# Local and strided attention with two feed-forward layers on one core: attention blocks 1 to 6 in another order, and the first weight conversions moved by a block

## The chip, the cores and the metric

The kernel runs on 1 core of one Trainium2 chip. The metric is device time in microseconds (us) of one execution. A median over runs is given for the kernel before; the profile comes from one execution whose own time is given beside its span.

## The reference

Three layers follow each other. Only the first lines matter here, since the change sits in the attention and in what the first feed-forward layer starts on.

```python
scores = scale * np.matmul(q, k.transpose(0, 1, 3, 2))      # batch 4, 8 heads, 576 positions, 64 wide
mask_local = (rel >= 0) & (rel < 32)                         # heads 0 to 3
mask_strided = (rel >= 0) & (pos[None, :] % 32 == pos[:, None] % 32)   # heads 4 to 7
attn = np.exp(scores - np.max(scores)); attn = attn / (np.sum(attn) + 1e-09)
x = matmul(attn, v)                  # becomes 2304 tokens x 512
h = x @ w_in;  g = h * np.tanh(softplus(h));  x = g @ w_out            # 512 -> 2048 -> 512
out = (silu(x @ w_gate) * (x @ w_val)) @ w_out2                        # 512 -> 1536 -> 512
```

## The kernel before, in words

**Precision.** The matrix products of the two feed-forward layers are done in three parts. Each operand is held as a high part (a cast, on ScalarE, L105) and a low part (the operand less its high part, on VectorE or GpSimd, L110). `mm3` (L112) issues three matmuls: high by high, high by low, low by high. Such a group is called a triple here. The low part of the weight is read by the third matmul only, and the low part of the input by the second only.

**Weights.** The weights arrive as 64-bit numbers and are converted. One weight tile takes four steps (`w_ops`, L195): a (a Square on ScalarE, L237, and a shift on VectorE, L238), b (L241), c (L244) and d (L247). Step d also asks for the next raw tile over SP's queue (`w_load`, L157). Then `w_hi` (L184) casts the high part on ScalarE and `w_lo` (L176) subtracts the low part on VectorE. `w_step(n)` (L255) issues the next n of these steps. The four tiles 0 to 3 hold the first quarter of `w_in`.

**Attention.** There are 24 steps (L297), each with six or eight blocks of 64 queries for two heads at once. Steps 0 to 2 and 6 to 8 are local (96 keys), steps 3 to 5 strided (64 keys). The work of a step is spread over four blocks of the program, which run as a pipeline: block a (`at_pair`, L537) issues scores (`at_qk`, TensorE), minima (`at_max`, VectorE) and exponentials (`at_exp`, ScalarE) of step a; sum and normalisation of step a-1 (`at_add`, `at_norm`: a reciprocal on VectorE, the rest on GpSimd); transposes and their copies of step a-2 (`at_tr`, `at_copy`); the product with v, the cast and the low part of step a-3 (`at_pv`, `at_hi` on ScalarE, `at_lo` on VectorE). What `at_hi` and `at_lo` write is x, the input of the first feed-forward layer. Minima, exponentials, transposes and copies come in two halves. The product with v has one PSUM buffer, so `at_pv` of a step waits for `at_lo` of the step before it; the scores have one pair of buffers, so `at_qk` waits for the minima of the block before.

**The order.** Every engine runs its instructions in the order of the program. The list `PAIR` (L506) gives the order within a block: load, transposes and copy of the first half, add, norm, product with v, load of v, `at_hi`, `at_whi` (the weight cast), scores, minima and exponentials of the first half, `at_conv`, `at_lo`, minima, transposes, copy and exponentials of the second half, `at_wlo` (the low part of the weight). For the blocks in `SC_FIRST` (1, 2, 3) the five entries in `SCORES` (L528) come first. Copies of the first half go to ScalarE for steps 2, 3 and 4 (`COPY_ACT`) and to VectorE otherwise; those of the second half always go to ScalarE.

**Between the blocks.** Behind block k the loop at L896 issues `KEEP[k]` filler matmuls on zeros (`spin`, L860; four of them behind blocks 2, 3 and 4), then `WSTEPS[k]` conversion steps, then the triples listed in `GROUPS[k]`. A triple (n, f, kc) belongs to column tile f of part n of the first layer and takes rows kc of x, which is head pair kc: head pairs 0 and 1 come from steps 0 to 2, 2 and 3 from steps 3 to 5. For n = 0 it reads weight tile f // 2 + 2 (kc // 2): tile 0 is read by the triples (0, 0 or 1, 0 or 1), tile 1 by (0, 2 or 3, 0 or 1), tile 2 by (0, 0 or 1, 2 or 3), tile 3 by (0, 2 or 3, 2 or 3).

Of the kernel before, what the change touches and what calls it, by code (L numbers as in the profile page):

```python
# [46 lines left out]
for _f in (0, 2):  # L47
# [26 lines left out]
}  # L74
CONV_FIRST = {3: 4}
COPY_ACT = (2, 3, 4)
WSTEPS = (0, 0, 0, 0, 4, 4, 2, 2, 1, 1, 2, 2, 2, 2, 2)
WFILL = 4
PAIR_AT = (0, 14, 17, 20, 23, 26, 29, 32, 36, 41, 46, 50)
SC_FIRST = (1, 2, 3)  # L80
WF = 8
DO2 = 6

# [2 lines left out]
def local_strided_attention__mish_moe__swiglu_kernel(  # L86
# [168 lines left out]
    def w_step(n):  # L255
        for _ in range(n):
            if not wq:
                wq.extend(w_ops())
            if wq:
                wq.pop(0)()  # L260
# [239 lines left out]
    def of(do, h):  # L500
        return lambda s: do(s, h)

    def at_conv(s):
        w_step(CONV_FIRST.get(s, 0))

    PAIR = [  # L506
        (at_load, 0),
        (of(at_tr, 0), -2),
# [7 lines left out]
        (at_qk, 0),  # L516
        (of(at_max, 0), 0),
        (of(at_exp, 0), 0),
        (at_conv, 0),
        (at_lo, -3),  # L520
        (of(at_max, 1), 0),
        (of(at_tr, 1), -2),
# [1 line left out]
        (of(at_exp, 1), 0),  # L524
        (at_wlo, 0),
    ]
    SPLIT, EXP0, COPY1, EXP1 = 9, 11, 16, 17
    SCORES = [9, 10, EXP0, 14, EXP1]  # L528
    apos = [0]

    rest = []
# [1 line left out]
    def at_rest():  # L533
        while rest:
            rest.pop(0)()

    def at_pair(split=False, later=()):  # L537
        at_rest()
        a = apos[0]
        if a < NS + 3:  # L540
            apos[0] += 1
            order = list(range(len(PAIR)))
            if a in SC_FIRST:
                order = SCORES + [x for x in order if x not in SCORES]
            for x in order:
                do, lag = PAIR[x]
                if 0 <= a + lag < NS:
                    if x in later:
                        held.append(lambda do=do, s=a + lag: do(s))
                    elif split and x >= SPLIT:  # L550
                        rest.append(lambda do=do, s=a + lag: do(s))
                    else:
                        do(a + lag)
# [54 lines left out]
    def do(n=None):  # L608
        for _ in range(len(todo) if n is None else min(n, len(todo))):
            todo.pop(0)()  # L610
# [246 lines left out]
    with tc.manual_schedule():  # L857
        nc.gpsimd.memset(wz, 0.0)

        def spin(n):  # L860
            if not n:
                return
            wp = ps.tile([128, 512], F32, tag="mm", name="wp", bufs=3)
            for _ in range(n):
                nc.tensor.matmul(
                    wp, lhsT=wz[:, :128], rhs=wz.unsqueeze(1).to_broadcast([128, 2, 256]), start=True, stop=True
                )
# [27 lines left out]

        for k in range(len(WSTEPS)):  # L896
            at_pair()
            spin(KEEP.get(k, 0))
            w_step(WSTEPS[k])
            for x in GROUPS.get(k, ()):  # L900
                g1_step(*x)
                if x == (1, 0, 3):
                    for f in range(QF):
                        act_m(0, (f,))
                        g_hi(0, f)
# [11 lines left out]
        def fill():  # L917
            at_rest()
            if fills[0] in PAIR_AT:
                at_pair(apos[0] >= NS, () if fills[0] else LATER)  # L920
            for x in MISH[fills[0]] if fills[0] < len(MISH) else ():
                x()
            fills[0] += 1
            do(3 if len(todo) > 10 else 2 if len(todo) > DO2 else 1)
# [21 lines left out]
        while apos[0] < NS + 3:  # L946
            at_pair()
# [183 lines left out]
```

## Time and profile before

| what | value |
|---|---|
| median of 3 runs | 883.16 us (882.87 to 883.2) |
| the profiled execution, its own time | 883.37 us |
| its span in the trace | 881.5 us |
| TensorE busy | 871.1 us of the span (99%) |
| VectorE, ScalarE, GpSimd busy | 66%, 43%, 16% of the span |

The span is the time from the first to the last instruction; the execution's own time lies 1.87 us above it. The busy share of TensorE includes the filler matmuls, and the ends of its matmuls are modelled.

### The profile page before, as it was taken

To read this page: it belongs to the slowest core of one execution; us is meant where nothing else is said; L and a number is where in the kernel's file an instruction comes from. 1 tells how busy PE (TensorE), PEld (TensorE's weight loads), DVE (VectorE), ACT (ScalarE), POOL (GpSimd) and SP (SyncE) were. 2 spreads that over 40 slices of the span, in tenths; PEclk is the share of its full clock that TensorE was granted. 3 is DMA by queue.
4 is the path that set the end of the run, shared out by engine and by line. 5 is a ranking of instruction groups with operands and counts; after the bars stand their busy time and mean duration, and the time that the engine had idled before them with its cause. 6 is when DMAs were issued, how large, how long until landed. Compare 5 with 4: busy or idle time off the path is not lost.

```text
span 881.5 us, 14233 instructions
## 1 busy us (share of the span) xinstructions
PE 871.1 (99%) x5284; PEld 727.6 (83%) x5284; DVE 582.5 (66%) x1269; ACT 381.1 (43%) x943; POOL 137.0 (16%) x156
## 2 busy tenths in 40 slices
PE   7999999999999999999999999999999999999998
PEld 4787888888888888888888888888888888888886
DVE  5898786688767977696485897764545635333534
ACT  6899763364334444353334544342333322332230
POOL 3332310000000000000122331211314212111211
PEclk9999999999999999999999999999999999999999
DMA  8775523355433544251048879666160573554222
GB/s 285 236 261 174 158 75 127 112 175 202 150 119 105 194 182 161 80 188 72 1 154 329 298 301 353 233 241 234 72 220 25 191 271 113 189 191 145 94 95 96
DMA packets 46292, 152.15 MB, mean 173 GB/s; under 512 B 5008, under 2 KB 8976, under 8 KB 46224
## 3 DMA queue, kind: packets, MB, share of 16 engines
q1 hardware_dynamic: 45936, 150.93, 48.6%
q8 instruction: 42, 0.69, 0.3%
q10 hardware_dynamic: 288, 0.31, 0.1%
q14 instruction: 26, 0.21, 0.1%
HBM read 115.05 MB, written 36.18 MB: 172 GB/s over the span
## 4 chain that ended last, share of the span: by engine, by line
PE 96%; DVE 2%; DMA 0%; ACT 0%; issue 0%; POOL 0%; ACTq 0%; DVEq 0%
PE y L114 23%; PE h L114 22%; PE o L114 17%; PE cXg L114 7%; PE cXv L114 7%; PE c L114 4%; PE cZv L114 4%; PE cZg L114 4%; PE xp L449 2%; PE cYv L114 2%; PE cYg L114 2%; PE sc L348 2%; PE tp L420 1%; DVE pt L373 1%; DMA cst<-in_consts_dram 0%; DVE wtmp L241 0%
## 5 line engine op out<-in xcount | busy, mean ns | idle before, releaser
L114 PE MATMUL y<-g,w 128*128 128x512 f32 (+1 forms) x960 | 202.8, 369 | 0.0
L114 PEld LDWEIGHTS y<-g,w 128*128 128x128 f32 x960 | 166.8, 189 | 30.7 <-DVE w L110 0.4
L114 PE MATMUL h<-xh,w 128*128 128x512 f32 (+1 forms) x640 | 188.4, 371 | 0.0
L114 PE MATMUL o<-wr,fs 128*128 128x512 f32 x648 | 149.6, 389 | 0.0
L114 PEld LDWEIGHTS o<-wr,fs 128*128 128x128 f32 x648 | 121.3, 188 | 25.0
L114 PEld LDWEIGHTS h<-xh,w 128*128 128x128 f32 x640 | 116.3, 189 | 20.6
L114 PE MATMUL h<-xl,w 128*128 128x512 f32 (+1 forms) x320 | 118.3, 370 | 1.7 <-DVE xl L110 1.7
L593 ACT ACTIVATE u<-h 128x512 f32<-128x512 f32 (+1 forms) x68 | 37.3, 548 | 142.4 <-PE h L114 142.4
L852 DVE TENSOR_TENSOR acc<-acc,o 128x512 f32<-128x512 f32 x90 | 61.4, 686 | 48.6 <-PE o L114 48.5
L110 POOL TENSOR_TENSOR fs<-k,fs 128x512 fp32r<-128x512 f32 x36 | 48.7, 1352 | 267.1 <-ACT fs L105 208.4
L114 PEld LDWEIGHTS h<-xl,w 128*128 128x128 f32 x320 | 60.4, 189 | 12.5 <-DVE xl L110 3.0
L110 DVE TENSOR_TENSOR g<-u,g 128x512 fp32r<-128x512 f32 (+1 forms) x80 | 51.1, 659 | 14.8 <-ACT g L105 14.8
L105 ACT CAST fs<-k 128x512 fp32r<-128x512 f32 x36 | 22.4, 622 | 88.2 <-DVE k L807 37.6
L389 ACT ACTIVATE pt<-pt,sm 128x64 f32<-128x64 f32 (+1 forms) x160 | 55.6, 350 | 8.5 <-DVE sm L373 7.9
L793 DVE TENSOR_TENSOR k<-cZg,k 128x512 f32<-128x512 f32 x12 | 8.3, 692 | 73.1 <-PE cZg L114 73.1
L110 POOL TENSOR_TENSOR B<-acc,B 128x512 fp32r<-128x512 f32 x6 | 8.4, 1392 | 301.2 <-ACT B L105 301.2
L114 PE MATMUL cXg<-T,wr 128*128 128x512 f32 x216 | 54.8, 389 | 0.0
L114 PE MATMUL cXv<-T,wr 128*128 128x512 f32 x216 | 54.8, 389 | 0.0
L105 ACT CAST ws<-wt 128x512 fp32r<-128x512 f32 x60 | 37.0, 616 | 35.9 <-DVE wt L247 31.7
L105 ACT CAST g<-u 128x512 fp32r<-128x512 f32 (+1 forms) x80 | 44.5, 574 | 15.6 <-PE y L114 15.4
L114 PEld LDWEIGHTS cXv<-T,wr 128*128 128x128 f32 x216 | 40.5, 188 | 8.4
L114 PEld LDWEIGHTS cXg<-T,wr 128*128 128x128 f32 x216 | 40.5, 188 | 8.5 <-DVE k L793 0.2
(102 smaller groups left out, 1314.9 us busy)
## 6 DMA issues: line engine op xcount, KB each, us to landing
raw<-in_w_dram SPq DMA_DIRECT2D x54, 512.0 KB, 3.7
wr<-wd_g_S SPq DMA_DIRECT2D x24, 512.0 KB, 7.2
wr<-wd_v_S SPq DMA_DIRECT2D x24, 512.0 KB, 7.3
wr<-wd_p SPq DMA_DIRECT2D x24, 512.0 KB, 4.5
wr<-wd_g_W SPq DMA_DIRECT2D x18, 512.0 KB, 6.3
wr<-wd_v_W SPq DMA_DIRECT2D x18, 512.0 KB, 7.1
rawl<-in_w_dram SPq DMA_DIRECT2D x14, 512.0 KB, 5.6
wd_g_W<-ws SPq DMA_DIRECT2D x12, 512.0 KB, 3.1
```

The lines of the kernel that those rows point to most:

```text
L105: nc.scalar.copy(hi, src)
L110: eng.tensor_tensor(out=lo, in0=src, in1=hi.bitcast(F32), op=ALU.subtract)
L114: nc.tensor.matmul(o, lhsT=lhs, rhs=rhs, start=first and i == 0, stop=last and i == 2, skip_group_check=more)
L348: nc.tensor.matmul(sc[h][x % 2 * 64:x % 2 * 64 + 64, x // 2 * w:(x // 2 + 1) * w], lhsT=t[64 * h:64 * h + 64, q0:q0 + 64], rhs=t[64 * h:64 ...
L373: nc.vector.tensor_tensor_reduce(pt[:, x], sc[h][:, t * w:(t + 1) * w], m, -0.125, 3.0e38, ALU.add, ALU.min, accum_out=sm[:, 0, x:x + 1],)
L389: nc.scalar.activation(out=pt[:, x], in_=pt[:, x], func=AF.Exp, scale=-1.0, bias=sm[:, 0, x:x + 1], accum_out=sm[:, 1, x:x + 1],)
L420: nc.tensor.transpose(tp[:, 128 * x:128 * x + 128], a, ident)
L449: nc.tensor.matmul(xp[64 * h:64 * h + 64, o:o + nq - skip], lhsT=vt[:, y % n, 64 * h:64 * h + 64], rhs=ts[:, c0 + skip:c0 + nq], start=Tru ...
L593: nc.scalar.activation(out=u, in_=p, func=AF.Mish)
L793: nc.vector.tensor_tensor(out=t, in0=p, in1=t, op=ALU.add)
L852: nc.vector.tensor_tensor(out=acc[c][:, t], in0=acc[c][:, t], in1=o, op=ALU.add)
```

## The change

Blocks 1 to 6 take one fixed order: load, weight cast, scores, minima and exponentials of the first half, minima of the second half, low part of the weight, transposes and copy of the first half, add, norm, product with v, load of v, cast of x, exponentials of the second half, low part of x, transposes and copy of the second half. `at_conv` is gone: weight tile 0, converted within block 3 before, is converted behind block 4, tile 1 behind block 5, tile 2 behind block 6, tile 3 in two halves behind blocks 7 and 8. From block 8 on the triples are dealt out anew: (0,2,2), the first to read tile 3, goes from block 8 to block 9, and one triple each moves on to blocks 10 and 11. The number of steps and of triples stays.

```diff
-    8: ((0, 0, 3), (0, 1, 3), (0, 2, 2)),
-    9: ((0, 2, 3), (0, 3, 0), (0, 3, 1)),
-    10: ((0, 3, 2), (0, 3, 3), (1, 0, 0)),
-    11: ((1, 1, 0), (1, 2, 0)),
+    8: ((0, 0, 3), (0, 1, 3)),
+    9: ((0, 2, 2), (0, 2, 3), (0, 3, 0)),
+    10: ((0, 3, 1), (0, 3, 2), (0, 3, 3)),
+    11: ((1, 0, 0), (1, 1, 0), (1, 2, 0)),
...
-CONV_FIRST = {3: 4}
 COPY_ACT = (2, 3, 4)
-WSTEPS = (0, 0, 0, 0, 4, 4, 2, 2, 1, 1, 2, 2, 2, 2, 2)
+WSTEPS = (0, 0, 0, 0, 4, 4, 4, 2, 2, 2, 2, 2, 2, 2, 2)
...
-SC_FIRST = (1, 2, 3)
+SC_FIRST = (1, 2, 3, 4, 5, 6)
...
-    def at_conv(s):
-        w_step(CONV_FIRST.get(s, 0))
-
...
-        (at_conv, 0),
...
-    SPLIT, EXP0, COPY1, EXP1 = 9, 11, 16, 17
-    SCORES = [9, 10, EXP0, 14, EXP1]
+    SPLIT, EXP0, COPY1, EXP1 = 9, 11, 15, 16
+    SCORES = [0, 8, 9, 10, EXP0, 13, 17, 1, 2, 3, 4, 5, 6, 7, EXP1, 12, 14, COPY1]
...
-                order = SCORES + [x for x in order if x not in SCORES]
+                order = SCORES
```

## Rows read from the trace of the kernel before

**Rows 1.** Stretches: us, length, busy of five engines, PEclk, DMA share, GB/s.

```profile
10.00:20.00 10.00, 7.58 (x134) 5.41 (x132) 6.81 (x32) 7.58 (x37) 5.33 (x9) 0.89 0.91 279
30.00:40.00 10.00, 8.67 (x129) 6.62 (x129) 9.48 (x55) 8.70 (x41) 4.47 (x8) 1.00 0.92 280
40.00:50.00 10.00, 10.00 (x150) 8.18 (x149) 7.08 (x44) 9.09 (x44) 2.96 (x6) 1.00 0.69 233
220.00:881.00 661.00, 657.85 (x3173) 555.94 (x3171) 410.27 (x652) 236.12 (x428) 96.83 (x78) 1.00 0.47 170
```

**Rows 2.** Waits of TensorE, first 60 us: total, times, longest.

```profile
PE xp L449 <- DVE xl L110: 2.1, 1, 2.1
PE h L114 <- DVE xl L110: 1.7, 3, 0.7
```

**Rows 3.** Timeline of TensorE: start, length, what, idle time before it.

```profile
13.87 1.03 PE L865 MATMUL wp<-wz 128*128 128x512 bf16 x4
...
17.69 1.45 PE L449 MATMUL xp<-ts,v 96*64 96x64 f32 x24 [2.09 <-DVE xl L110]
19.07 1.13 PE L348 MATMUL sc<-qk 64*64 64x64 f32 x32
...
22.32 0.92 PE L449 MATMUL xp<-ts,v 96*64 96x64 f32 x24
...
36.06 0.60 PE L420 MATMUL tp<-cst,pt 128*96 128x128 f32 x4
...
43.36 0.47 PE L114 MATMUL h<-xh,w 128*128 128x512 f32 x1
...
45.52 0.60 PE L420 MATMUL tp<-cst,pt 128*96 128x128 f32 x4
```

**Rows 4.** Stretches of half a microsecond around that wait.

```profile
17.50:18.00 0.50, 0.31 (x8) 0.31 (x10) 0.24 (x2) 0.00 (x0) 0.11 (x1) 0.85 0.85 295
18.00:18.50 0.50, 0.50 (x15) 0.50 (x12) 0.00 (x0) 0.00 (x0) 0.50 (x2) 0.50 0.87 279
...
21.00:21.50 0.50, 0.50 (x3) 0.25 (x2) 0.50 (x4) 0.50 (x4) 0.00 (x0) 0.74 1.00 411
```

**Rows 5.** Timeline of VectorE.

```profile
14.25 1.20 DVE L241 SCALAR_TENSOR_TENSOR wtmp<-raw,wtmp 128x512 int32<-128x512 int32 x1
...
22.61 0.42 DVE L238 TENSOR_SCALAR wtmp<-raw 128x512 int32<-128x512 int32 x1
...
25.20 0.20 DVE L405 RECIPROCAL sm<-sm 128x8 f32<-128x8 f32 x1
...
29.95 0.22 DVE L373 CUSTOM_DVE_ANT_0 pt<-sc,cst 128x96 f32<-128x96 f32 x1
...
30.44 0.67 DVE L110 TENSOR_TENSOR xl<-xp,xh 128x384 fp32r<-128x384 f32 x2
...
31.55 0.69 DVE L110 TENSOR_TENSOR w<-wtmp,w 128x512 fp32r<-128x512 f32 x1
...
43.30 0.23 DVE L373 CUSTOM_DVE_ANT_0 pt<-sc,cst 128x64 f32<-128x64 f32 x1 [0.70 <-PE sc L348]
...
44.92 0.69 DVE L241 SCALAR_TENSOR_TENSOR wtmp<-raw,wtmp 128x512 int32<-128x512 int32 x1
```

**Rows 6.** Timeline of ScalarE.

```profile
13.67 0.34 ACT L389 ACTIVATE pt<-pt,sm 128x64 f32<-128x64 f32 x1
...
14.99 0.46 ACT L105 CAST xh<-xp 128x384 fp32r<-128x384 f32 x1
...
19.18 0.60 ACT L105 CAST xh<-xp 128x128 fp32r<-128x128 f32 x3 [2.42 <-PE xp L449]
...
24.09 0.57 ACT L428 COPY ts<-tp 128x512 f32<-128x512 f32 x1
...
25.31 0.62 ACT L105 CAST w<-wtmp 128x512 fp32r<-128x512 f32 x1 [0.22 <-DVE wtmp L247]
```

**Rows 7.** DMA issued between 6.4 and 6.9 us: size, us to landing.

```profile
qk<-in_qk_dram SPq DMA_DIRECT2D x1, 280.0 KB, 8.2
```

## The prediction
> **What bounds the kernel now.** I read the busy times by stretch first. From 40 us on TensorE has no idle time within a stretch like the third row, and between 220 and 881 us it is idle for 3.15 us of 661 [rows 1]. So the end is set by when TensorE gets through its first 40 us: a delay or a gain there, in blocks 3 to 9, moves the end by as much. In the stretch from 10 to 20 us it is idle for 2.42 us, from 30 to 40 for 1.33 [rows 1]. The table of waits names the two causes: 2.1 us once, when the product with v waits for the low part of x of the step before, and three waits of 1.7 in all, of triples for the low part of x [rows 2]. The timeline places the first: idle for 2.09 us ahead of 17.69, and the scores of step 4 follow only at 19.07, since they stand behind that product [rows 3]. Last I read the granted clock: 0.85 in the half microsecond from 17.5, then 0.50 until about 21.25 (0.74 in the slice from 21.0) [rows 4]. That is the 1.2 GHz level, for some 3.4 us after the long idle time; the 24 small matmuls at 17.69 take 1.45 there and 0.92 at 22.32 [rows 3].
>
> **What the change removes.** The idle 2.09 us come from VectorE's order in block 3: the four conversion steps of tile 0 stand ahead of the low part of x. With them gone, and x's cast put ahead of the second half of the exponentials, the cast need not wait until 14.99 but can run from about 13.7, where the first half ends [rows 6] and the product with v is over (the fillers behind it start at 13.87 [rows 3]). Cast 0.46 and low part about 0.55 give 14.7. TensorE ends its four fillers at 13.87 + 1.03 = 14.9 [rows 3] and begins the scores of step 4 there, not at 19.07: **4.2 us ahead**. Their data are in: the load of the second head pair's first part needs 8.2 us from about 6.4 [rows 7], so 14.6. With no idle time the clock should stay at its upper level as well.
>
> **What it adds: a chain through ScalarE and VectorE.** Now follow blocks 4 to 6. The low part of x stands on VectorE directly ahead of the conversion, and waits for x's cast, which stands on ScalarE behind the weight cast, the first exponentials and a copy. Durations: an exponential 0.33 (four from 13.67 to 14.99), a copy about 0.5 and a weight cast 0.55 to 0.62, an x cast 0.46 to 0.60 [rows 6]; a low part of x about 0.6, a conversion 25.20 - 22.61 = 2.6 [rows 5].
> - Block 4: scores 14.9 to 15.6 (0.6 to 0.7, from the 1.13 at the lower clock [rows 3]); exponentials from 15.9, four to 17.2; copy to 17.8; x cast to 18.4; low part to 19.0; conversion of tile 0 to 21.6. VectorE idles for over a microsecond ahead of 18.4. TensorE: product with v of step 1, transposes, fillers, scores of step 5, done near 19; then it waits for ScalarE's late copy (it stands behind the second exponentials, to about 20), and for tile 0.
> - Block 5: minima can't start before 21.6, as they stand behind the conversion. Weight cast to 22.2, three exponentials to 23.3, copy 23.8, x cast 24.3, low part 24.9, conversion of tile 1 to 27.5. One link is 0.6 + 1.0 + 0.5 + 0.5 + 0.1 + 0.6 + 2.6 = 5.9.
> - Block 6: the same link, so tile 2 is converted by 33.4. Before, VectorE took 4.75 us from one block's minima to the next (25.20 to 29.95), and tile 2's low part was subtracted at 31.55 [rows 5].
> - Block 7 has the old order, with the weight's low part at its end. Copy and reciprocal to 34.1; minima, low part of x, minima, low part of the weight as from 29.95 to 31.55 + 0.69, 2.3 [rows 5], to 36.4. The first triple's third matmul needs it; it and the three of the second triple take 4 x 0.24 (nine in 45.52 - 43.36 [rows 3]), to 37.4. Before, block 8 began at 36.06 [rows 3]: **1.3 us late**. The lead of 4.2 us is spent.
> - Block 8 has the same order and waits as before; its third triple only moves on. The 1.3 stay.
> - Block 9: its first triple now reads tile 3, whose low part is the last of VectorE's work in this block. Minima and low part of x last there from 43.30 to 44.92, and the weight's low part of 0.69 would end at 45.6; the third matmul is due at 43.36 + 2 x 0.24 = 43.84 [rows 3, 5]. **1.8 us more**; nothing is queued on TensorE that could pass it. This wait can't be under about 1.6 and can grow if VectorE is late.
>
> So TensorE is 3.1 us late at block 9, and behind it no idle time is left to take that in [rows 1]. Edits that I cost at nothing: the moved triples and conversion steps keep their number. On SP's queue the load of keys stands ahead of the values' load in every block from 4 on, as before; a raw tile, asked for by step d, now follows a block later, at about 21 for tile 2 and 27 for tile 3, yet over 9 us ahead of its use, against the 8.2 of [rows 7]. What stands behind such a request (the keys of the next pair) has a block more. On GpSimd sum and normalisation follow the reciprocal, now behind the weight's low part, in the time in which VectorE waits for x's cast; their transposes are due 2 us later. If that cover went, TensorE would wait at the transposes, by up to a microsecond.
>
> **The clock.** In block 7 TensorE waits from about 32.7 to 36.4 with two matmuls in it. Before, idle time of 2.09 us brought the clock to 1.2 GHz, while waits of up to 0.7 us left it at 1.00 between 30 and 40 us [rows 1 to 4]; the new wait is nearer to the first. Some 3.4 us at half rate lose up to 1.7 us. Block 8 is on the path (its minima wait for its scores), so I charge 1.5; the bounds are 0 and, with a second fall behind block 9's wait, 3.4. A fall in block 5 would be hidden, for there VectorE ends last. The Trainium skill says in "TensorE: Matmul & The Clock Gate", section "HAM oscillation — how this bites in real kernels", that TensorE is throttled while it waits between bursts and that the next burst starts slow; by it this change pays for its waits a second time, 4.6 and not 3.1, and [rows 4] bear it out for one wait and [rows 1] speak against it for short ones.
>
> **The price of a conversion.** Step b took 1.20 us at 14.25 and 0.69 at 44.92 [rows 5]; the first lies in a stretch in which GpSimd is busy more than half the time [rows 1]. In the new order the normalisation falls ahead of the conversion, so I take the 2.6 of the conversion at 22.61 [rows 5]; 0.5 more for each of three, 1.5, is the upper bound. "SBUF — State Buffer" in the Trainium skill, section "Who interferes with whom", says that a VectorE instruction with two inputs in SBUF and a GpSimd instruction that reads SBUF shut each other out; if the two met here, the sum would be 6.1 and not 4.6.
>
> **Sum.** 3.1 + 1.5 = 4.6 us on the profiled 883.37: 888.0; the median of the runs is 0.21 lower, so 887.8.
>
> **Rivals.**
> - *No fall of the clock*: 3.1 alone, 886.3. For it: in block 7 two matmuls and the scores before them interrupt the wait. Chance 0.20.
> - *Two falls*, in blocks 7 and 9: 6.3, 889.5. Chance 0.12.
> - *Gain and waits cancel*: VectorE's own work in a link is 2.6 + 0.6 + 1.0 + 0.6 + 0.1 = 4.9 (conversion, low part of x, minima, low part of the weight, reciprocal). Were ScalarE never waited for, tile 2 would be converted by 31.4 and block 7 over at 35.4, 0.7 early; with block 9's 1.8 that is 1.1 late, 884.3. Chance 0.13.
> - *Faster*: the lead of 4.2 us lasts through block 7. The place is the third matmul of its first triple: if the low part of tile 2 is subtracted by 31 and not 36.4, TensorE never waits there; 4.2 less block 9's 1.8 is a gain of 2.4, 880.8. For it: TensorE's own work is short in these blocks and its old waits were small [rows 2]. Against it: even two links of 4.9 end later, so block 4 would have to be 2 us shorter too. The point is a low part of tile 2 by 33.3: block 7 then ends at 34.3, 1.8 early, which pays for block 9's wait. Chance 0.07.
>
> **Numbers.** My forecast has 0.48; with its neighbours without a fall or with two, slower by over 0.2% (1.77 us, about what a measurement of this kernel can tell from no change) has 0.80, within it 0.13, faster 0.07. I hold the chain uncertain by 0.4 us in each of blocks 4, 5 and 6, 1.2 in all, the clock by 1.5 below and 1.9 above. So the range reaches from 0.8 below the cancelling case, 883.5, to 890.2, 0.7 above the case with two falls.
>
> **What would show it.** Right: scores of step 4 near 15; no wait of 2 us for a low part of x; waits of TensorE on the weight's cast and low part (rows PE or PEld h <- ACT w, DVE w) of 1 us and more in blocks 5 and 7, and one near 1.8 in block 9; VectorE's minima of blocks 5 to 7 some 5.9 us apart; a granted clock of 0.5 in a stretch behind block 7. Wrong: if tile 2's low part is done before TensorE asks for it, or block 8 begins before 36, the chain is shorter than I put it; if the clock stays at 1.00 the price is 3.1 alone.

## The result, and the profile after

The changed kernel takes 888.49 us, the median of six executions (886.45 to 889.63), against 883.01: a ratio of 1.0058, with a 95% interval of 1.0044 to 1.0071. It is slower by 5.5 us, clear of noise. The forecast was 887.8, in a range of 883.5 to 890.2. The profiled execution took 888.43 us with a span of 886.6, 5.1 above that of before. The six are not alike: two of them, at 886.51 and 886.45, have a mean granted clock of 1.000, the four at 888.4 to 889.6 one of 0.995 or 0.996.

Lines in the code are now one to five lower (the matmul of `mm3` was L114 and is L113, the subtraction was L110 and is L109). Stretches of the changed kernel, columns as in [rows 1]:

```profile
10.00:20.00 10.00, 9.71 (x179) 6.54 (x178) 6.59 (x53) 9.87 (x54) 4.65 (x10) 1.00 0.95 294
20.00:30.00 10.00, 8.28 (x96) 6.06 (x91) 8.26 (x37) 7.07 (x27) 2.24 (x4) 0.83 0.68 238
30.00:40.00 10.00, 7.54 (x81) 5.32 (x81) 7.24 (x28) 6.42 (x28) 3.65 (x6) 0.83 0.72 240
40.00:50.00 10.00, 8.18 (x128) 6.06 (x125) 7.57 (x40) 8.70 (x38) 3.07 (x6) 1.00 0.57 166
220.00:886.00 666.00, 663.00 (x3195) 560.17 (x3194) 412.98 (x658) 239.88 (x435) 96.89 (x78) 1.00 0.47 170
```

The stretch from 20 to 30 us before, which [rows 1] leave out:

```profile
20.00:30.00 10.00, 9.33 (x139) 6.90 (x134) 9.40 (x46) 9.09 (x40) 2.42 (x4) 0.94 0.67 234
```

The stretch from 10 to 20 us has gained: TensorE is idle for 0.29 us there, 2.42 before. The three behind it have 1.72, 2.46 and 1.82 us of idle time, where there were 0.67, 1.33 and none before, and in two of them the clock is at 0.83. The rest of the program is as it was (3.0 us idle from 220 us on, 3.15 before). So the time went in blocks 5 to 9.

The waits of TensorE, first 70 us, as in [rows 2]:

```profile
PE h L113 <- ACT w L104: 2.9, 2, 1.7
PE h L113 <- DVE w L109: 2.3, 2, 1.2
...
PE h L113 <- DVE xl L109: 0.5, 1, 0.5
```

The wait of the product with v for the low part of x is gone, and two of the three short ones. In their place stand four waits for weights, 5.2 us: two for the cast, two for the low part. The timeline of TensorE has their places, as in [rows 3]:

```profile
15.03 0.70 PE L347 MATMUL sc<-qk 64*64 64x64 f32 x32
...
22.64 0.57 PE L113 MATMUL h<-xh,w 128*128 128x512 f32 x1 [1.69 <-ACT w L104]
...
34.56 0.51 PE L113 MATMUL h<-xh,w 128*128 128x512 f32 x1 [1.23 <-ACT w L104]
...
36.80 1.22 PE L113 MATMUL h<-xh,w 128*128 128x512 f32 x2 [1.12 <-DVE w L109]
...
38.67 1.05 PE L419 MATMUL tp<-cst,pt 128*96 128x128 f32 x4
...
43.69 0.60 PE L419 MATMUL tp<-cst,pt 128*96 128x128 f32 x4
...
48.18 0.73 PE L113 MATMUL h<-xh,w 128*128 128x512 f32 x2 [1.21 <-DVE w L109]
...
49.90 0.60 PE L419 MATMUL tp<-cst,pt 128*96 128x128 f32 x4
```

Scores of step 4 at 15.03, 4.0 us ahead; block 5 waits for tile 0 until 22.64; block 7 for tile 2 until 36.80; block 8 begins at 38.67 and not 36.06; block 9 waits for tile 3 until 48.18. In the kernel before block 9 begins at 41.17 and block 10 at 45.52:

```profile
41.17 0.60 PE L420 MATMUL tp<-cst,pt 128*96 128x128 f32 x4
```

VectorE shows the chain that leads there (its low parts of x, the first minima of blocks 5, 6 and 7, and the two late low parts of weights):

```profile
14.44 0.56 DVE L109 TENSOR_TENSOR xl<-xp,xh 128x384 fp32r<-128x384 f32 x1 [0.33 <-ACT xh L104]
...
18.66 0.69 DVE L109 TENSOR_TENSOR xl<-xp,xh 128x128 fp32r<-128x128 f32 x3 [1.52 <-ACT xh L104]
...
21.85 0.22 DVE L372 CUSTOM_DVE_ANT_0 pt<-sc,cst 128x64 f32<-128x64 f32 x1
...
24.53 0.62 DVE L109 TENSOR_TENSOR xl<-xp,xh 128x320 fp32r<-128x320 f32 x2 [1.01 <-ACT xh L104]
...
28.06 0.26 DVE L372 CUSTOM_DVE_ANT_0 pt<-sc,cst 128x96 f32<-128x96 f32 x1 [0.33 <-PE sc L347]
...
30.60 0.67 DVE L109 TENSOR_TENSOR xl<-xp,xh 128x384 fp32r<-128x384 f32 x2 [0.68 <-ACT xh L104]
...
34.34 0.22 DVE L372 CUSTOM_DVE_ANT_0 pt<-sc,cst 128x96 f32<-128x96 f32 x1
...
36.06 0.69 DVE L109 TENSOR_TENSOR w<-wtmp,w 128x512 fp32r<-128x512 f32 x1
...
47.44 0.69 DVE L109 TENSOR_TENSOR w<-wtmp,w 128x512 fp32r<-128x512 f32 x1
```

From 18.66 to 24.53 to 30.60 is 5.9 and 6.1 us a block, and each time VectorE has waited for x's cast. The first minima of blocks 5, 6 and 7 lie 6.2 and 6.3 us apart. The clock, in stretches of two microseconds:

```profile
22.00:24.00 2.00, 1.36 (x3) 0.80 (x4) 1.51 (x14) 2.00 (x9) 0.34 (x1) 0.73 0.86 243
24.00:26.00 2.00, 2.00 (x6) 1.56 (x5) 1.44 (x4) 2.00 (x10) 1.20 (x3) 0.50 0.94 348
...
36.00:38.00 2.00, 1.20 (x3) 1.01 (x4) 1.78 (x5) 1.57 (x7) 0.74 (x1) 0.65 0.96 360
38.00:40.00 2.00, 2.00 (x13) 1.30 (x13) 0.24 (x1) 0.00 (x0) 0.00 (x0) 0.50 1.04 373
```

It fell twice, behind the wait of block 5 and behind those of block 7, and not behind that of block 9.

### The profile page after: what moved, and what is told of

Read it like the earlier page. It is cut to its first block, busy times and chain, and to the rows that moved or that the text cites. A ratio compares the mean times of both kernels' runs of the same rounds, so it can differ in the third digit from the quotient of the medians.

```text
span 886.6 us, 14231 instructions
## 1 busy us (share of the span) xinstructions
PE 875.0 (99%) x5284; PEld 728.9 (82%) x5284; DVE 582.4 (66%) x1269; ACT 381.1 (43%) x943; POOL 136.5 (15%) x156
## 4 chain that ended last, share of the span: by engine, by line
PE 96%; DVE 2%; ACT 1%; issue 0%; POOL 0%; DVEq 0%; ACTq 0%; POOLq 0%
PE y L113 22%; PE h L113 22%; PE o L113 17%; PE cXg L113 7%; PE cXv L113 7%; PE c L113 4%; PE cZv L113 4%; PE cZg L113 4%; PE xp L448 2%; PE cYv L113 2%; PE cYg L113 2%; PE sc L347 2%; PE tp L419 1%; DVE pt L372 1%; PE wp L860 0%; ACT pt L388 0%
## 5 line engine op out<-in xcount | busy, mean ns | idle before, releaser
L113 PE MATMUL y<-g,w 128*128 128x512 f32 (+1 forms) x960 | 202.9, 369 | 0.0
L113 PE MATMUL h<-xh,w 128*128 128x512 f32 (+1 forms) x640 | 190.5, 375 | 5.4 <-ACT w L104 2.9
L113 PEld LDWEIGHTS y<-g,w 128*128 128x128 f32 x960 | 166.8, 189 | 30.8 <-DVE w L109 0.4
L113 PE MATMUL o<-wr,fs 128*128 128x512 f32 x648 | 149.6, 389 | 0.0
L113 PEld LDWEIGHTS o<-wr,fs 128*128 128x128 f32 x648 | 121.3, 188 | 25.0
L113 PEld LDWEIGHTS h<-xh,w 128*128 128x128 f32 x640 | 117.1, 190 | 27.7 <-ACT w L104 3.6
L113 PE MATMUL h<-xl,w 128*128 128x512 f32 (+1 forms) x320 | 119.1, 372 | 0.6 <-DVE xl L109 0.5
L109 POOL TENSOR_TENSOR fs<-k,fs 128x512 fp32r<-128x512 f32 x36 | 48.7, 1353 | 267.0 <-ACT fs L104 208.4
L113 PEld LDWEIGHTS h<-xl,w 128*128 128x128 f32 x320 | 60.8, 190 | 11.2 <-DVE xl L109 1.7
L109 DVE TENSOR_TENSOR g<-u,g 128x512 fp32r<-128x512 f32 (+1 forms) x80 | 51.1, 659 | 14.8 <-ACT g L104 14.8
L113 PE MATMUL cXg<-T,wr 128*128 128x512 f32 x216 | 54.8, 389 | 0.0
L113 PE MATMUL cXv<-T,wr 128*128 128x512 f32 x216 | 54.8, 389 | 0.0
L109 POOL TENSOR_TENSOR B<-acc,B 128x512 fp32r<-128x512 f32 x6 | 8.3, 1391 | 301.2 <-ACT B L104 301.2
L113 PEld LDWEIGHTS cXg<-T,wr 128*128 128x128 f32 x216 | 40.5, 188 | 8.5 <-DVE k L788 0.2
L113 PEld LDWEIGHTS cXv<-T,wr 128*128 128x128 f32 x216 | 40.5, 188 | 8.4
```

The source lines that it names most:

```text
L109: eng.tensor_tensor(out=lo, in0=src, in1=hi.bitcast(F32), op=ALU.subtract)
L113: nc.tensor.matmul(o, lhsT=lhs, rhs=rhs, start=first and i == 0, stop=last and i == 2, skip_group_check=more)
```

## The experiments

Theory A is the prediction's. Theory B lays the whole loss on the new order of blocks 4 to 6, theory C on the clock. Each time has its ratio to the kernel before on the same chip; the medians of the kernel before there are 882.7 to 882.9 us.

**The order alone.** Edit to the changed kernel (triples as before):

```diff
-WSTEPS = (0, 0, 0, 0, 4, 4, 4, 2, 2, 2, 2, 2, 2, 2, 2)
+WSTEPS = (0, 0, 0, 4, 4, 4, 2, 2, 1, 1, 2, 2, 2, 2, 2)
```

> The new order of blocks 1 to 6 alone: weight tile 0 is converted behind block 3, and the other conversions and the triples stay where they were in the kernel before. Theory A (weights a block too late for the order in which their low parts are made, and a chain over ScalarE and VectorE of 5.9 us a block): tile 2's low part is ready in block 6, so TensorE waits for no low part of a weight in blocks 7 and 9; the chain still costs the lead of 4 us by block 7; about 884 us, within 1.5 us of before. Theory B (the new order of blocks 4 to 6 is the whole loss, wherever the weights are converted): 887 to 888.5 us, like the changed kernel. Theory C (the loss is the clock, which falls when TensorE idles): 883 if the granted clock stays at 1.00, else 885 and more.

885.39 us (884.88 to 885.95), ratio 1.003 (1.0019 to 1.004). No wait for a weight is left in its table of waits. A misses by 1.4, B by 1.6 or more. C had 885 and more with a fall of the clock, and that number fits; but the one run with a mean clock of 1.000 took 884.88, where C had 883, so the clock isn't the whole loss. The order costs something with the weights early, and the late weights cost the rest.

**The weights alone.** Edit to the kernel before (triples as in the changed kernel):

```diff
-CONV_FIRST = {3: 4}
+CONV_FIRST = {}
-WSTEPS = (0, 0, 0, 0, 4, 4, 2, 2, 1, 1, 2, 2, 2, 2, 2)
+WSTEPS = (0, 0, 0, 0, 4, 4, 4, 2, 2, 2, 2, 2, 2, 2, 2)
```

> The old order of all blocks, with the conversions and triples of the changed kernel (tile 0 behind block 4, and so on). Theory A: the idle 2.09 us ahead of the product with v shrink (low part of x at 15.5 to 16.0 and not 17.1), but block 7 still waits for the low part of tile 2 and block 9 for that of tile 3, 1.5 to 1.8 us: 884 to 885 us. Theory B (the order alone costs): 881 to 883 us, since VectorE's conversion no longer stands ahead of the low part of x. Theory C: as the clock goes, 882 with 1.00 throughout.

891.89 us (890.08 to 892.51), ratio 1.01 (1.0087 to 1.0114): every theory missed, and the changed kernel is faster than this. Its waits of TensorE, and the minima of blocks 6, 7 and 8 on VectorE:

```profile
PE h L114 <- DVE w L110: 4.2, 4, 1.2
PE h L114 <- ACT w L105: 2.9, 3, 1.7
```

```profile
31.39 0.26 DVE L373 CUSTOM_DVE_ANT_0 pt<-sc,cst 128x96 f32<-128x96 f32 x1 [3.62 <-PE sc L348]
...
37.08 0.26 DVE L373 CUSTOM_DVE_ANT_0 pt<-sc,cst 128x96 f32<-128x96 f32 x1 [0.20 <-PE sc L348]
...
42.75 0.26 DVE L373 CUSTOM_DVE_ANT_0 pt<-sc,cst 128x96 f32<-128x96 f32 x1 [0.71 <-PE sc L348]
```

I had followed VectorE alone. Here each engine waits for the other in turn: the triples wait for the weight's low part at the end of VectorE's block, the next scores stand behind the triples, and the next minima (and all behind them) wait for those scores. The blocks come 5.7 us apart. This is theory D. From 31.39 to 37.08 VectorE waits for scores for 0.20 us only, so there its own work sets the pace; the waits of 3.62 and 0.71 are where the loop shows.

**The low part early in the old order too.** Edit to the kernel of the run before this one:

```diff
             if a in SC_FIRST:
                 order = SCORES + [x for x in order if x not in SCORES]
+            elif 5 <= a <= 9:
+                order = [0, 1, 2, 3, 4, 5, 6, 7, 8, 9, 10, EXP0, 18, 12, 13, 14, 15, COPY1, EXP1]
```

> The old order with the conversions and triples of the changed kernel, as in the run with the weights alone, but with the weight's low part directly behind the minima of the first half in blocks 5 to 9. Theory D (TensorE and VectorE wait for each other in turn: scores, minima, low parts, then the triples, and behind them the next scores): each of blocks 5, 6, 7 and 9 is 1.0 us shorter, 4 in all: 887.5 to 888 us. Rival (what costs there is the conversion's distance, or ScalarE's weight cast): 890.5 or more.

888.85 us (888.42 to 890.19), ratio 1.0067 (1.0053 to 1.008): 3.0 us back, not 4. The waits for the weight's low part fall from 4.2 us to 0.2; those for its cast grow from 2.9 to 3.8, those for low parts of x from 0.5 to 1.6. D holds in the main. It also tells what the new order of the changed kernel is good for: with weights a block late, an early low part is worth some 3 us.

**The low part early in blocks 7 to 9 as well.** Edit to the changed kernel:

```diff
                 order = SCORES
+            elif a in (7, 8, 9):
+                order = [0, 1, 2, 3, 4, 5, 6, 7, 8, 9, 10, EXP0, 17, 12, 13, 14, COPY1, EXP1]
```

> The changed kernel, with the weight's low part directly behind the minima of the first half in blocks 7, 8 and 9 too. Theory A: the waits of 1.1 us for it in block 7 and 1.2 us in block 9 fall by 0.9 and 1.2 us, and with the first of them shorter the clock may stay up: 886.4 us with a fall of the clock, 884.5 without. Theory B: no difference beyond 0.5 us, 888.5. Theory C: a gain only if the granted clock rises by it.

887.45 us (886.50 to 890.28), ratio 1.0057 (1.0044 to 1.0069): the median is 1.0 less, where A had 2.1, and by the ratio the run isn't told apart from the changed kernel (1.0058). What the edit does is read from the trace. Block 9's wait fell to 0.2, and the block takes 47.93 - 42.76 = 5.2 us, 6.2 in the changed kernel. In block 7 the gain was eaten: the triples now wait 1.14 for the low part of x, which comes behind, and the weight's low part meets GpSimd's normalisation and takes 1.11 us, not 0.69. VectorE and GpSimd in that block:

```profile
34.39 1.11 DVE L109 TENSOR_TENSOR w<-wtmp,w 128x512 fp32r<-128x512 f32 x1
```

```profile
34.12 1.74 POOL L407 TENSOR_TENSOR pt<-pt,sm 128x384 f32<-128x384 f32 x2 [2.13 <-DVE sm L372]
```

GpSimd's pair takes 1.29 elsewhere in this kernel. This is the rule of "SBUF — State Buffer" in the Trainium skill, section "Who interferes with whom" (two inputs in SBUF against a GpSimd instruction that reads SBUF); the trace agrees, 0.42 and 0.45 us.

**Tile 3's first triple last in block 9.** Edit to the changed kernel:

```diff
-    9: ((0, 2, 2), (0, 2, 3), (0, 3, 0)),
-    10: ((0, 3, 1), (0, 3, 2), (0, 3, 3)),
+    9: ((0, 3, 0), (0, 3, 1), (0, 2, 2)),
+    10: ((0, 2, 3), (0, 3, 2), (0, 3, 3)),
```

> The changed kernel, with block 9's triples in the order (0,3,0), (0,3,1), (0,2,2), so that two triples of tile 1, 1.4 us, come ahead of the first that reads tile 3; (0,2,3) goes to block 10. Theory A: block 9's wait for the low part of tile 3 goes almost wholly, 1.4 us less: 887.1 us, other waits and the clock as in the changed kernel. Theory B: no difference beyond 0.5 us, 888.5. Theory C: none, for the clock did not fall in block 9.

887.29 us (885.22 to 887.89), ratio 1.0049 (1.0036 to 1.0061). TensorE's wait for tile 3 is down to 0.21:

```profile
46.36 0.50 PE L113 MATMUL h<-xh,w 128*128 128x512 f32 x1 [0.21 <-DVE w L109]
```

The median is 1.2 lower, with intervals of the ratio that overlap. The one run of the five with a clock of 1.000 took 885.22, the two such runs of the changed kernel 886.5: 1.3; and block 9 takes 46.70 - 41.87 = 4.8 us, 1.4 less. A holds; B and C have no such term. That one run is the profiled one. Its waits in blocks 5 and 7 are those of the changed kernel, and yet its clock stays at 1.00 (its row in the table of waits, then stretches):

```profile
PE h L113 <- ACT w L104: 2.9, 2, 1.7
```

```profile
20.00:25.00 5.00, 3.04 (x22) 1.86 (x23) 3.85 (x20) 3.83 (x16) 1.47 (x3) 1.00 0.60 193
...
35.00:40.00 5.00, 3.88 (x60) 2.81 (x59) 3.60 (x18) 2.69 (x14) 2.19 (x5) 1.00 0.99 343
```

**Fillers where TensorE waits.** Edit to the changed kernel (the fillers behind blocks 5 and 7 use another PSUM buffer):

```diff
-KEEP = {0: 2, 1: 3, 2: 4, 3: 4, 4: 4}
+KEEP = {0: 2, 1: 3, 2: 4, 3: 4, 4: 4, 5: 6, 7: 4}
```

> The changed kernel, with six filler matmuls more behind block 5's scores and four behind block 7's, 1.45 and 0.96 us, in times in which TensorE waits for a weight's cast (1.7 and 1.2 us). Nothing else waits for them. Theory A: the granted clock stays at 1.00, and every run takes 886.5 us, as those two runs of the changed kernel did in which it was 1.00; the waits for weights stay. Theory C (the clock is the whole loss): 883. If the clock is no cause at all, 888.5 as before.

887.70 us (886.64 to 889.77), ratio 1.0055 (1.0043 to 1.0067). By its ratio the run isn't told apart from the changed kernel; the clock is sized from its profiled execution. There the clock stayed at 1.00 in all stretches, and blocks 8, 9 and 10 begin at:

```profile
37.65 0.60 PE L419 MATMUL tp<-cst,pt 128*96 128x128 f32 x4
...
42.08 0.60 PE L419 MATMUL tp<-cst,pt 128*96 128x128 f32 x4
...
48.30 0.60 PE L419 MATMUL tp<-cst,pt 128*96 128x128 f32 x4
```

It took 886.84 us with a span of 885.0, 1.6 less than the changed kernel's, and has the same waits for low parts of weights, 2.3 us. That sizes the clock: 1.6 us, so C falls. A had every run at 886.5, and only two of the five came there (886.64 and 886.84). One took 887.70 with a mean clock of 1.000, so it is 0.9 us longer for another reason than the clock. Two took 887.75 and 889.77 with 0.999 and 0.998; since 0.998 is also the mean of the kernel before in the execution with the one fall of [rows 4], a fall may be part of it there. There is no profile of these three, and what lengthened them stays open.

**Three edits together**: fillers, tile 3 last, low part early.

> The changed kernel with three edits of other runs together: the weight's low part early in blocks 7 to 9, block 9's triples of tile 1 ahead of tile 3's, and fillers in blocks 5 and 7. Theory A: 888.5 less 2.0 for the clock, 1.4 for block 9 and 0.3 to 0.9 for block 7: 884.2 to 884.8 us, every run alike. If the waits replace each other, 885.5 or more.

884.99 us (884.37 to 885.84), ratio 1.0023 (1.0014 to 1.0033). The sum holds within 0.8 us: 3.5 us of the loss go with those edits. Over the kernel before 2.2 us are left. In the profiled execution (885.84, the longest of the nine) block 8 begins at 37.27, 1.2 us behind 36.06; that much is in the chain of blocks 4 to 6. One wait of 0.9 us stands behind 400 us; the rest isn't traced.

**The conversion behind block 3, and no more.** Edit to the kernel before:

```diff
-CONV_FIRST = {3: 4}
+CONV_FIRST = {}
-WSTEPS = (0, 0, 0, 0, 4, 4, 2, 2, 1, 1, 2, 2, 2, 2, 2)
+WSTEPS = (0, 0, 0, 4, 4, 4, 2, 2, 1, 1, 2, 2, 2, 2, 2)
```

> The kernel before, with tile 0's conversion behind block 3 and not within it, and no other edit: x's cast still waits behind all exponentials of block 3. Theory A: low part of x at 15.5 to 16.0, conversion to 18.6, minima of block 4 at 18.7 and not 20.25, a gain of 1.5: 881.2 us. Rival: 882.7.

884.07 us (882.05 to 886.89), ratio 1.0015 (1.0005 to 1.0024). The median is above both forecasts. The profiled execution is the fastest, and does what A said: block 8 begins at 34.67, 1.4 us ahead of before. The others take up to 4.8 us more, and none of them was profiled; the next run shows what may be the cause.

**The front alone.** The kernel of the run with the order alone, with the new order in blocks 1 to 3 only:

```diff
-SC_FIRST = (1, 2, 3, 4, 5, 6)
+SC_FIRST = (1, 2, 3)
```

> The new order in blocks 1 to 3 alone, tile 0 converted behind block 3, all else as in the kernel before: the low part of x ahead of the conversion, and x's cast between the exponentials. Theory A (the lead is real, and it is the order of blocks 4 to 6 with the weights a block late that spends it): VectorE's minima of block 4 begin at 17.5 and not 20.25, and the 2.7 us last: 880.3 us. Rival (VectorE's own work sets the pace of blocks 4 to 8, and a lead in block 4 only turns into waits of TensorE): 882.7, no change.

883.54 us (881.57 to 886.08), ratio 1.001 (1.000 to 1.002), again with a wide spread and with a median above both forecasts. The profiled execution is one of the slowest (886.08), and TensorE's timeline says why:

```profile
31.92 1.14 PE L448 MATMUL xp<-ts,v 128*64 128x54 f32 x32 [2.48 <-DMA v<-in_v_str_dram]
```

The lead was there up to 29.4, and then the values of step 4 had not landed. A new bound: the loads. They had been asked for at 22.96, behind a raw tile and keys, and took 8.8 us. (SP's queue, start and length.)

```profile
22.06 0.33 SPq L168 DMA_DIRECT2D raw<-in_w_dram  x1
22.44 0.42 SPq L327 DMA_DIRECT2D qk<-in_qk_dram  x1
22.96 0.39 SPq L334 DMA_DIRECT2D v<-in_v_str_dram  x1
```

The same load of values here, and in the kernel before (where it was asked for at 25.46, with the same two requests ahead of it; size, us to landing):

```profile
v<-in_v_str_dram SPq DMA_DIRECT2D x1, 512.0 KB, 8.8
```

```profile
v<-in_v_str_dram SPq DMA_DIRECT2D x1, 512.0 KB, 6.5
```

In the kernel before the values land at about 32.0, and the product that reads them begins at 32.08: this load had no slack to begin with. Here it is asked for at 22.96, and TensorE comes to its product at 29.4, so 6.5 us would just do and 8.8 are 2.3 too many. What made it slower in this execution isn't shown.

**The front, with the values first.** Edit to the run before (the raw tile's request waits in a counter and goes out behind the keys):

```diff
             wpend.append((key, w, tf))
-            w_load()
+            if apos[0] <= 9:
+                due[0] += 1
+            else:
+                w_load()
...
             load_qk(i)
+        while due[0]:
+            due[0] -= 1
+            w_load()
...
+            if a <= 9:
+                order = [x for x in order if x]
+                order.insert(order.index(6) + 1, 0)
```

> The new order in blocks 1 to 3 alone with tile 0 converted behind block 3, and in blocks 1 to 9 the requests on SP's queue in another order: the values for the product with v first, then the keys, and only then the raw weight tile that the conversion asked for. Theory A with its front gain: in the run with the front alone TensorE waited 2.5 us for values that were asked for at 23 us behind a raw tile and keys, and landed at 31.9. With the values first they land by 28, TensorE does not wait for them, and the lead of 2.6 us in block 6 lasts: 880.3 to 881.5 us, and the runs lie closer together. Rival (DMA is full from 20 to 35 us and any order is late somewhere): 883 to 884, with a wait for keys or raw weights in place of the one for values.

**880.57 us** (880.39 to 880.79), ratio 0.997 (0.9959 to 0.9982): faster than both kernels, and its six runs lie within 0.4 us. The same three requests:

```profile
20.61 0.33 SPq L338 DMA_DIRECT2D v<-in_v_str_dram  x1
20.99 0.42 SPq L331 DMA_DIRECT2D qk<-in_qk_dram  x1
21.88 0.33 SPq L168 DMA_DIRECT2D raw<-in_w_dram  x1
```

The values land at 25.9, 5.3 us after their request:

```profile
v<-in_v_str_dram SPq DMA_DIRECT2D x1, 512.0 KB, 5.3
```

Block 8 begins at 33.23 and not 36.06, and no wait for a load is left in TensorE's table. The median is 2.3 us under that of the kernel before beside it (882.87), the span 2.8 under (878.7 against 881.5): the front gain, forecast as 2.6, is shown. No run has the requests in this order without the new front; TensorE's table of the kernel before has no wait for values that such a run could take away.

**The new order in blocks 4 to 6 on top.** Edit to that kernel:

```diff
-SC_FIRST = (1, 2, 3)
+SC_FIRST = (1, 2, 3, 4, 5, 6)
```

> The run with the front and the values first, with the new order in blocks 4 to 6 as well, and no other edit: what this order costs by itself, with the weights early and the loads in time. Theory A: VectorE waits for x's cast in each of blocks 4 to 6, 0.7 to 1.1 us, since the cast stands on ScalarE behind the exponentials and a copy, and TensorE comes to block 8 2.5 to 3 us later: 883.0 to 883.6 us, up to 885 if the clock falls. Rival (the order alone was held up by late values in the run with the order alone, and costs nothing now): 880.6.

886.02 us (885.15 to 887.29), ratio 1.0037 (1.0022 to 1.0051): 5.4 us more, and A had 2.5 to 3, or 4.4 with a fall of the clock. VectorE's waits for x's cast are as A has them:

```profile
20.74 0.69 DVE L109 TENSOR_TENSOR xl<-xp,xh 128x128 fp32r<-128x128 f32 x3 [1.10 <-ACT xh L104]
...
26.60 0.62 DVE L109 TENSOR_TENSOR xl<-xp,xh 128x320 fp32r<-128x320 f32 x2 [1.01 <-ACT xh L104]
...
33.23 0.67 DVE L109 TENSOR_TENSOR xl<-xp,xh 128x384 fp32r<-128x384 f32 x2 [0.68 <-ACT xh L104]
```

They make 2.8 us. TensorE waits for the same cast in block 5, 1.89 us, its clock falls (0.69 from 25 to 30 us), the scores of block 6 come late for that, and VectorE waits 0.89 for them. Block 8 begins at 38.16, 4.9 us behind the 33.23 of the run without. With the requests in the old order the run with the order alone took 885.39, so late values weren't what held it. So the order alone is dear once the weights are early.

**The low part of x ahead of the minima** in blocks 5, 7 and 8 of the fastest kernel:

```diff
                 order = SCORES
+            elif a in (5, 7, 8):
+                order = [0, 1, 2, 3, 4, 5, 6, 7, 8, 9, 12, 10, EXP0, 13, 14, COPY1, EXP1, 17]
```

> The run with the front and the values first, with the low part of x ahead of the minima of the first half in blocks 5, 7 and 8, where TensorE still waits 0.5 to 0.6 us for it. Theory A (these waits are on the path): up to 1.5 us less, 879.1 to 879.6 us. Rival (the minima and exponentials come 0.6 us later for it, and the next block's low parts with them): 880.6, no change.

880.37 us (880.12 to 883.12), ratio 0.9977 (0.9968 to 0.9986): not told apart from 880.57, with two of eleven runs at 883.1. TensorE's waits for the low part of x fall from 1.6 to 0.2 us, but block 8 begins at 33.10 and not 33.23: the minima come later by most of it, as the rival had it. The span is 878.2 against 878.7, so 0.5 of A's 1.5 us may be there; the times don't tell.

## Why the prediction was right

- **What bounds the kernel**: right. All 5.1 us of the span came in blocks 4 to 9, and nothing behind them took any of it in: block 10 begins at 49.90 and not 45.52, 4.4 us late, with one triple of 0.7 us fewer done by then.
- **The lead**: 4.2 us forecast, 4.0 measured (15.03 against 19.07 of [rows 3]). That it is worth something where the rest keeps up is shown by the run with the front and the values first.
- **The chain**: 5.9 us a block forecast, 5.9 and 6.1 measured from one low part of x to the next; low parts of x at 18.4 and 24.3 forecast, and with the link of 5.9 at 30.2, 18.66, 24.53 and 30.60 measured. The minima, which the prediction named as the sign, lie 6.2 and 6.3 us apart and not 5.9. The run with the new order in blocks 4 to 6 on top shows the mechanism apart from the late weights.
- **Block 7**: 1.3 us late was forecast. Without a fall of the clock (the run with fillers) block 8 begins at 37.65, 1.6 late.
- **Block 9**: 1.8 us. In that run the block takes 48.30 - 42.08 = 6.2 us, and 45.52 - 41.17 = 4.35 for as many triples before: 1.9. The 1.21 in brackets in the timeline understates it. In the changed kernel the first matmul of the block's triples comes at 46.24, 0.54 us after the transposes ahead of it and not 0.18 as before, right behind the cast of tile 3, which ends at 46.18; the prediction had no such term. And the matmul ahead of the wait for the low part has a modelled end. Moving the triple gave 1.2 to 1.4 back.
- **The clock**: 1.5 us charged for one fall, 1.6 measured. It fell in block 5 too, which the prediction held possible and hidden: in the run with fillers block 6's low part of x comes at 30.43, 0.17 earlier, so it nearly was (VectorE waited 0.33 us for the scores at 28.06). That it fell at all is in part luck: in two of the six runs the mean clock is 1.000, and in the run with tile 3 last the same waits left it at 1.00. Why it falls in one execution and not in another stays open.
- **The sum**: 4.6 forecast, 5.1 in the profiled execution (2.6 at the start of block 8, 0.6 more in block 8 at the lower clock, 1.9 in block 9). The rival without a fall, 886.3, is what two of the six runs did: 886.5.
- **The conversion's price**: 21.85 - 19.26 = 2.6 behind block 4, not lengthened, as taken.
- Two readings were wrong, and nothing in the sum hangs on them. The 4.75 us from minima to minima start from the reciprocal at 25.20; the minima begin at 25.31, so it is 4.64. And the wait of 0.7 us that left the clock up stands at 26.23; those between 30 and 40 us are 0.34 to 0.50. The case of two falls counts 3.2 us for the clock, the bound 3.4.
- Weak points, found by the runs: the loads were costed at nothing, which holds for the changed kernel alone; where the lead lasts, they become the bound. And I treated VectorE's chain as if scores were always there; the run with the weights alone shows a loop over both engines, and the expectation for it was 7 us too low.

## What to carry to other kernels

When work is moved to a later block, ask for each product of it where in that block it is finished, and who reads it there; here TensorE was 4.0 us ahead at the scores of step 4, 1.8 at those of step 6 (27.29 against 29.10) and 0.6 at those of step 7 (32.60 against 33.15). An engine that runs in order should not get a cast for another engine behind work that itself waits (here x's cast behind the exponentials). And where a lead is won, look at the loads next: their requests have to be put in the order of their use.

## What was not expected of the hardware

The same load of 512 KB of values took 5.3, 6.5 and 8.8 us to land: asked for first; behind a raw tile and keys in the kernel before; and behind the same two in the profiled execution of the front alone. What made the last one slower is open. Its DMA engines were busy at 0.65 and moved 180 GB/s from 24 to 25 us, in its first microseconds, and those of the kernel before were nearly idle (0.02) just ahead of its requests; but the run with the conversion behind block 3 had them busy too (0.91, 352 GB/s), and its values took 6.5 us. With the values first the spread of the runs went from 4.5 to 0.4 us. That points to the loads and doesn't prove it: the two kernels ran on different chips, and with the same requests two of eleven runs of the last kernel took 883.1 us.

The clock fell behind waits of 1.23 and 1.12 us with two single matmuls between them (block 7), and not behind one of 1.21 us (block 9). The waits alone don't decide it: with waits of 1.69, 1.23 and 1.12 us in blocks 5 and 7 it stayed at 1.00 in the profiled execution of the run with tile 3 last. With four or six filler matmuls in the waits for the casts the mean clock was 0.998 or more in five runs of five; without them it was 0.996 or less in four of six.
